# One K^TV product moved behind an output tile, W' units spread singly, a thirteenth half-tile kept in SBUF

## Chip, cores, metric

The kernel runs on one core of a Trainium2 chip. The metric is the time of one execution in microseconds (us), lower is better. A *span* is the time from the first to the last instruction of the one execution that was traced; it is about 1.3 us shorter than the timed run.

## The reference, cut to what matters

Two linear-attention branches A and B work on the same input `x` (2048 x 640, bf16, 32 heads of 20) and are mixed by a gate.

```python
qkv = x @ wqkv;  pq, pk = phi(q), phi(k)      # phi: exp below zero, t + 1 above, plus 1e-6
kv  = einsum("bhsd,bhse->bhde", pk, v)        # K^TV, one 20 x 20 block for each head
z   = sum over s of pk
o   = (pq @ kv) / (pq . z + 1e-6)
branch = o @ wo
out = g * A + (1 - g) * B                     # g = sigmoid(sum(x * gate_w))
```

## The kernel before

The kernel never forms `v`. It computes G = K^T X ("g units"), transposes G by DMA, multiplies it by the V weights (K^TV), masks the result to the head blocks on VectorE, and multiplies by `wo` to get W' ("W' units": PE, a ScalarE copy, and a DMA that rearranges the rows). An output tile of 128 rows is phi(q), scaled by the gate and the denominator, times W'. Each half of it (one branch) takes ten matmuls.

A list scheduler in the kernel, with its own cost for each instruction, fixes the order on each engine. PE alone keeps the order of the program text. The scheduler also deals out the eight banks of PSUM.

```python
def kv_unit(X):                                   # K^TV
    for us in ((0, 1, 2, 3), (4, 5)):             # 20 matmuls, then 10
        ps = Buf("kv", "ps")                      # one PSUM bank for each group
        ...  e.matmul(PS[0:GR, ps.slot, GR*i : GR*i+GR], WV[X][:, c, lo:lo+GR], gv[...])       # L661
        op("DVE", ... tensor_tensor(out=KVL[X]..., in0=PS[0:GR, ps.slot, ...], in1=BDM ...))   # the mask, L676

def wp_unit(X, u):                                # W': PE (L697, L698), ScalarE copy (L711), DMA into WP
    ...
def den(X):                                       # denominators: 4 matmuls in 4 column groups (L826)
    ...  # then ScalarE copies them from PSUM (L845), VectorE takes reciprocals (L855),
         # DMAs broadcast them, VectorE scales the phi(q) tiles (L891)

def o_part(t):                                    # first branch's half: PE (L913), ScalarE copy to OA[t] (L937)
def o_rest(t):                                    # second branch's half: PE (L913), VectorE adds OA[t] (L950)
def out_unit(t):                                  # both halves accumulated in PSUM, ScalarE copy (L959)
...
o_part(0); o_part(1); o_part(2)
den("B")
kv_unit("B")
o_part(3)
for u in range(NU):                               # NU = 6
    wp_unit("B", u)
    if u % 2:
        o_part(4 + u // 2)
for t in range(7, NOA):                           # NOA = 12
    o_part(t)
...
for t in range(NOA): o_rest(t)
for t in range(NOA, NT - 1): out_unit(t)
out_last(NT - 1)
```

`... ` and closing comments are cuts and notes of this document; `L` numbers are those of the profile.

Of the kernel before, what the change touches and what calls it, by code (L numbers as in the profile page):

```python
# [74 lines left out]
class Sched:  # L75
# [7 lines left out]
    def op(self, eng, fn, cost, ins=(), outs=(), after=(), prio=None, name="", dma=None):  # L83
        o = Op(eng, fn, cost, list(ins), list(outs), after, len(self.ops) if prio is None else prio, name, dma)
        self.ops.append(o)
        return o
# [165 lines left out]
def body(nc, A_x, A_wqkv, A_wo, B_x, B_wqkv, B_wo, gate_w, out, log=None):  # L252
# [6 lines left out]
    bf, f32 = dt.bfloat16, dt.float32  # L259
# [11 lines left out]
    PK = {X: sb("PK" + X, [128, NT * D], bf) for X in XS}  # L271
# [22 lines left out]
    GSf = GS["A"][:, :, :].rearrange("p c f -> p (c f)")  # L294
    PQ["B", 3] = GSf[:, 0:2560].rearrange("p (g s) -> p g s", g=NC)
    FXT = {"A": WV["A"][:, :, :].rearrange("p c f -> p (c f)")[:, 0:2048].rearrange("p (b s) -> p b s", b=NB), "B": XNf[:, 0:2048].rearrange("p (b s) -> p b s", b=NB)}
    NOA = 12
    OA = [XNf[:, 2048 + 1280 * i : 3328 + 1280 * i].bitcast(f32) for i in range(6)]
    OA += [PK["B"][:, 1280 * i : 1280 * i + 1280].bitcast(f32) for i in range(6)]
    NEK, NEQ, NOS = 4, 4, 4  # L300
    EK = sb("EK", [128, NEK, D], bf)
    EQ = EK[:, :, :].rearrange("p k f -> p (k f)")[:, 0 : NEQ * 512].rearrange("p (k f) -> p k f", k=NEQ)
# [27 lines left out]
    def psw(b, w):  # L330
        return PS[:, b.slot : b.slot + b.n, :].rearrange("p a b -> p (a b)")[:, 0:w]
# [15 lines left out]
    def mm_cost(n):  # L347
        return n / 2.4 + 2.5

    def act_cost(n):  # L350
        return 190 + 0.833 * n

    def dve1(n):
        return 155 + 1.04 * n
# [297 lines left out]
    def kv_unit(X):  # L652
        gv = GS[X][:, :, :].rearrange("p c (g m) -> p c g m", g=NC)
        for us in ((0, 1, 2, 3), (4, 5)):
            ps = Buf("kv", "ps")

            def fn(e, us=us, ps=ps):
                for i, u in enumerate(us):
                    lo = GR * u if u < 5 else D - GR
                    for c in range(NC):  # L660
                        r = e.matmul(  # L661
                            PS[0:GR, ps.slot, GR * i : GR * i + GR],
                            WV[X][:, c, lo : lo + GR],
                            gv[:, c, :, lo // 5 : lo // 5 + 24],
                            start=(c == 0),
                            stop=(c == NC - 1),
                        )
                return r

            op("PE", fn, 5 * len(us) * mm_cost(GR), ins=[bwv[X]] + [bgs[X, g] for g in range(NC)], outs=[ps], name="kv" + X)  # L670
            b = Buf("kvl")
            bkvl[X].append(b)
            n = len(us)
            op(
                "DVE",
                lambda e, us=us, ps=ps, n=n: e.tensor_tensor(  # L676
                    out=KVL[X][:, us[0] : us[0] + n, :].rearrange("p u (m g) -> p u g m", g=NC),
                    in0=PS[0:GR, ps.slot, 0 : GR * n].rearrange("p (u g m) -> p u g m", u=n, g=NC),
                    in1=BDM.unsqueeze(1).unsqueeze(1).to_broadcast([GR, n, NC, 24]),
                    op=ALU.mult,  # L680
                ),
                dve1(GR * n),
                ins=[ps, bcst],
                outs=[b],
                prio=-1,
                name="kvm",
            )
# [4 lines left out]
    def wp_unit(X, u):  # L692
        ps = Buf("wp", "ps", 2)

        def fn(e):
            a = psw(ps, D)
            e.matmul(a[0:GR, 0:512], KVL[X][:, u, :], WO[X][:, u, 0:512], start=True, stop=True)  # L697
            return e.matmul(a[0:GR, 512:D], KVL[X][:, u, :], WO[X][:, u, 512:D], start=True, stop=True)  # L698

        op(  # L700
            "PE",
            fn,
            mm_cost(512) + mm_cost(128),
            ins=[bkvl[X][u // 4], bwo[X] if u < 5 else bwo[X, 5]],
            outs=[ps],
            name="wp%s%d" % (X, u),
        )
        b = Buf("wst")
        op(
            "ACT",  # L710
            lambda e: e.activation(WST[X][:, u, :], psw(ps, D)[0:GR, :], ACT.Copy),  # L711
            act_cost(D),
            ins=[ps],
            outs=[b],
            prio=-1,
            name="wpc",
        )
        bwp[X, u] = b
        d = Buf("wpm")
        bwpm[X].append(d)  # L720
        r = 80 if u == 5 else 0
        lo, hi = GR * u, min(D, GR * u + GR)
        dma(
            "SP",
            "wpm%s%d" % (X, u),
            WP[X][lo // 5 : hi // 5, :, :],
            WST[X][r:GR, u, :],
            1280 * (hi - lo),
            ins=[b],
            outs=[d],  # L730
            issue=850.0,
            prio=-1,
        )
# [53 lines left out]
    def scale_now(X, b, h):  # L787
        pqs_op[X, b, h].prio = len(sch.ops)
# [116 lines left out]
    def o_mm(X, t, ps, lo, hi, first="A", last="B"):  # L905
        b = t // 4

        def fn(e):
            a = psw(ps, hi - lo)
            for g in range(NC):  # L910
                for l0 in range(lo, hi, 512):
                    h0 = min(hi, l0 + 512)
                    r = e.matmul(  # L913
                        a[:, l0 - lo : h0 - lo],
                        PQ[X, b][:, g, 128 * (t % 4) : 128 * (t % 4) + 128],
                        WP[X][:, g, l0:h0],
                        start=(X == first and g == 0),
                        stop=(X == last and g == NC - 1),
                    )
            return r  # L920

        op(
            "PE",
            fn,
            5 * sum(mm_cost(min(512, hi - l0)) for l0 in range(lo, hi, 512)),
            ins=[bfx[X, b, t % 4 // 2]] + bwpm[X],
            outs=[ps],
            name="o%s%d" % (X, t),
        )
# [3 lines left out]
    def o_part(t):  # L933
        ps, b = Buf("oa", "ps", 2), Buf("oas")
        boa[t] = b
        o_mm("A", t, ps, 0, D, last="A")
        op("ACT", lambda e: e.activation(OA[t], psw(ps, D), ACT.Copy), act_cost(D), ins=[ps], outs=[b], name="oac")  # L937

    def o_rest(t):
        ps = Buf("o", "ps", 2)  # L940
        o_mm("B", t, ps, 0, D, first="B")
        o_post(t, ps, 0, D, "ADD")
# [29 lines left out]
    def out_unit(t):  # L972
        ps = Buf("o", "ps", 2)
        for X in XS:
            o_mm(X, t, ps, 0, D)
        o_post(t, ps, 0, D, "ACT")
# [52 lines left out]
    o_part(1)  # L1029
    o_part(2)  # L1030
    den("B")
    kv_unit("B")
    o_part(3)
    for u in range(NU):
        wp_unit("B", u)
        if u % 2:
            o_part(4 + u // 2)
    for t in range(7, NOA):
        o_part(t)
    for b in range(3):  # L1040
        for h in range(2):
            scale_now("B", b, h)
    for t in range(NOA):
        o_rest(t)
    for h in range(2):
        scale_now("B", 3, h)
    for t in range(NOA, NT - 1):
        out_unit(t)
# [11 lines left out]
def bass_gated_mix__linear_attn_block__linear_attn_block__prompt_kernel(nc, *args):  # L1060
    body(nc, *args)
# [28 lines left out]
```

## Time and profile before

| | before |
|---|---|
| time, median of the first 3 runs | 191.1 us (190.75 to 191.29) |
| span of the traced execution | 189.5 us |
| PE busy | 184.9 us, 98% |
| denominator matmul of B starts | 143.83 us |
| last copy (VectorE, 128 columns) starts | 187.47 us |
| end of the span after that start | 2.04 us |

First, the page of the kernel before: the share of busy time (engine, busy us, share of the span, instructions), and the chain that ended last, by engine.

```profile
PE 184.9 (98%) x1245; PEld 108.1 (57%) x1269; DVE 127.4 (67%) x251; ACT 95.6 (50%) x171; POOL 0.4 (0%) x6
...
PE 98%; issue 1%; DVE 0%; DVEq 0%
```

PE (matmuls) is the limit. Its weight loads (PEld) run beside the matmuls. The list of waits of PE, before: who waited for whom, us in total, times, longest.

```profile
PE ps L425 <- DVE ONE L368: 1.1, 1, 1.1
PE ps L743 <- issue: 0.2, 1, 0.2
```

Next, the timeline of the stretch that the change rearranges, before. Columns: start, duration, engine, line, operation, output<-inputs, count; in brackets the idle time before it and what ended it.

```profile
143.83 0.40 PE L826 MATMUL ps<-TSH,CST 128*32 128x512 bf16 x4
...
144.16 1.89 PEld L661 LDWEIGHTS ps<-GSB,WVB 128*120 128x120 bf16 x30 [0.23 <-issue]
144.16 2.02 PE L661 MATMUL ps<-GSB,WVB 128*120 128x120 bf16 x30
144.54 0.83 ACT L845 ACTIVATE DTT<-ps,EPSC 128x256 f32<-128x256 f32 x2
145.04 0.95 DVE L855 RECIPROCAL RCT<-DTT 128x128 f32<-128x128 f32 x1 [1.45 <-ACT DTT L845]
145.91 2.10 DVE L676 TENSOR_TENSOR KVLB<-ps,CST 120x480 bf16<-120x480 f32 x2
...
147.45 0.13 PEld L697 LDWEIGHTS ps<-WOB,KVLB 120*120 120x120 bf16 x1 [0.25 <-issue]
147.48 0.40 PE L697 MATMUL ps<-WOB,KVLB 120*120 120x512 bf16 x1
```

From the denominator matmul (L826) PE goes to K^TV (L661), an output half-tile (not shown), and the first W' unit (L697). Denominator to first W' unit is 147.48 - 143.83 = 3.65 us. The "issue" entry of 0.2 us in the list of waits belongs to branch A's denominator matmul, at 106.2 us: the next matmul there (L743) starts 0.18 us late. Here PE shows no gap, but that is no proof that it did not wait: a matmul's end is modelled, and 120-column matmuls that start 0.055 us apart each carry a modelled duration of about 0.22 us, so a pause of up to 0.16 us between two of them stays covered.

### The profile page before, as it was taken

Reading aid. Unit: us, or ns where it says so; the run is one execution under the profiler, and the core shown is the slowest. Engines: PE = TensorE matmul, PEld = TensorE weight load, DVE = VectorE, ACT = ScalarE, POOL = GpSimd, SP = SyncE. Lnnn points to the kernel's source line nnn. Section 1 sums busy time; section 2 is a strip of 40 time slices with the busy share of each in tenths; the row PEclk is TensorE's granted clock in tenths of the full one; section 3 lists DMA queues with packets and bytes.
Section 4 is the critical chain, followed back from the end, with each engine's and each line's share of the span. In section 5 each row is a group of like instructions: output and inputs, shape, how many; then the busy total and the mean of one; then the engine's idle time right before and its main releaser. Section 6 shows DMA issues by size and latency. Waiting matters only on the chain.

```text
span 189.5 us, 3195 instructions
## 1 busy us (share of the span) xinstructions
PE 184.9 (98%) x1245; PEld 108.1 (57%) x1269; DVE 127.4 (67%) x251; ACT 95.6 (50%) x171; POOL 0.4 (0%) x6
## 2 busy tenths in 40 slices
PE   7999999999999999999999999999999999999995
PEld 3555555555565656655557556655666555555552
DVE  2389888888833546478787689888996935865300
ACT  2256565656554545544584777876624875000112
POOL 0000000000000000000000000000000000000000
PEclk9999999999999999999999999999999999999999
DMA  5979999999014011013010006330020053233312
GB/s 142 310 137 139 196 358 377 364 244 208 13 44 105 0 38 35 0 35 31 7 21 13 3 3 144 109 98 5 0 50 19 24 169 94 73 136 108 107 69 69
DMA packets 29469, 19.42 MB, mean 102 GB/s; under 512 B 17390, under 2 KB 29198, under 8 KB 29454
## 3 DMA queue, kind: packets, MB, share of 16 engines
q1 hardware_dynamic: 29300, 19.17, 39.2%
q8 instruction: 10, 0.16, 0.4%
q10 hardware_dynamic: 154, 0.05, 0.2%
q14 instruction: 5, 0.04, 0.1%
HBM read 9.95 MB, written 2.64 MB: 66 GB/s over the span
## 4 chain that ended last, share of the span: by engine, by line
PE 98%; issue 1%; DVE 0%; DVEq 0%
PE ps L913 23%; PE ps L743 22%; PE ps L620 18%; PE ps L491 18%; PE ps L492 5%; PE ps L621 5%; PE ps L661 2%; PE ps L425 1%; PE ps L697 1%; PE ps L438 1%; PE ps L698 0%; PE ps L826 0%; DVE TSB L957 0%; DVE ONE L368 0%; PE ps L472 0%
## 5 line engine op out<-in xcount | busy, mean ns | idle before, releaser
L491 PE MATMUL ps<-WKW,XT 128*128 128x512 bf16 x154 | 43.1, 380 | 0.0
L760 ACT ACTIVATE EK<-ps 128x512 bf16<-128x512 f32 x40 | 23.9, 599 | 31.3 <-PE ps L743 29.9
L492 PE MATMUL ps<-WKW,XT 128*128 128x128 bf16 (+1 forms) x160 | 35.2, 220 | 0.3
L524 ACT ACTIVATE EK<-ps 128x640 bf16<-128x640 f32 x32 | 22.3, 703 | 12.5 <-PE ps L492 6.1
L491 PEld LDWEIGHTS ps<-WKW,XT 128*128 128x128 bf16 x160 | 15.7, 98 | 19.0 <-issue 0.3
L743 PE MATMUL ps<-XT,WQA 128*128 128x512 bf16 x96 | 24.0, 379 | 0.1
L743 PE MATMUL ps<-XT,WQB 128*128 128x512 bf16 x95 | 23.3, 379 | 0.4 <-issue 0.2
L620 PE MATMUL ps<-XN,PKB 128*128 128x512 bf16 x80 | 23.5, 379 | 0.0
L770 DVE TENSOR_SCALAR EK<-EK 128x512 bf16<-128x512 bf16 x40 | 11.6, 291 | 17.2 <-ACT EK L760 17.0
L620 PE MATMUL ps<-XN,PKA 128*128 128x512 bf16 x78 | 23.1, 379 | 0.1
L621 PE MATMUL ps<-XN,PKA 128*128 128x129 bf16 x80 | 17.6, 220 | 0.1
L621 PE MATMUL ps<-XN,PKB 128*128 128x129 bf16 x80 | 17.6, 220 | 0.0
L913 PE MATMUL ps<-WPA,EX 128*128 128x128 bf16 (+1 forms) x116 | 16.8, 296 | 0.2
L913 PE MATMUL ps<-WPB,PKA 128*128 128x512 bf16 (+1 forms) x118 | 16.4, 298 | 0.1
L743 PEld LDWEIGHTS ps<-XT,WQB 128*128 128x128 bf16 x100 | 10.9, 118 | 8.5 <-issue 0.2
L492 PEld LDWEIGHTS ps<-WKW,XT 128*128 128x128 bf16 x160 | 15.7, 98 | 0.0
L743 PEld LDWEIGHTS ps<-XT,WQA 128*128 128x128 bf16 x100 | 10.6, 117 | 8.1
L527 DVE TENSOR_SCALAR EK<-EK 128x640 bf16<-128x640 bf16 x32 | 10.4, 325 | 7.0 <-ACT EK L524 7.0
L959 ACT ACTIVATE TSB<-ps 128x640 bf16<-128x640 f32 (+1 forms) x4 | 2.7, 677 | 23.9 <-PE ps L913 23.9
L620 PEld LDWEIGHTS ps<-XN,PKA 128*128 128x128 bf16 x80 | 9.4, 117 | 7.9
L620 PEld LDWEIGHTS ps<-XN,PKB 128*128 128x128 bf16 x80 | 9.4, 118 | 7.8
L535 DVE SCALAR_TENSOR_TENSOR PKA<-ps,EK 128x640 bf16<-128x640 f32 x16 | 13.2, 825 | 0.6
(77 smaller groups left out, 231.5 us busy)
## 6 DMA issues: line engine op xcount, KB each, us to landing
out_dram<-TSB SPq DMA_DIRECT2D x15, 160.0 KB, 1.8
XN<-in_A_x_dram SPq DMA_DIRECT2D x1, 2240.0 KB, 9.2
WKW<-in_A_wqkv_dram SPq DMA_DIRECT2D x5, 160.0 KB, 3.5
WKW<-in_B_wqkv_dram SPq DMA_DIRECT2D x5, 160.0 KB, 3.9
WQA<-in_A_wqkv_dram SPq DMA_DIRECT2D x1, 800.0 KB, 10.9
WQB<-in_B_wqkv_dram SPq DMA_DIRECT2D x1, 800.0 KB, 13.6
WVA<-in_A_wqkv_dram SPq DMA_DIRECT2D x1, 800.0 KB, 12.8
WVB<-in_B_wqkv_dram SPq DMA_DIRECT2D x1, 800.0 KB, 14.3
```

Source lines behind the costliest of these rows:

```text
L491: e.matmul(a[:, 0:512], l, WK[X][:, c, 0:512], start=(c == 0), stop=(c == NC - 1))
L492: return e.matmul(a[:, 512:w], l, WK[X][:, c, 512:w], start=(c == 0), stop=(c == NC - 1))
L524: op("ACT", lambda e: e.activation(EK[:, ek.slot, :], psw(ps, D), ACT.Exp), act_cost(D), ins=[ps] + first, outs=[ek], name="ke")
L527: lambda e: e.tensor_scalar(EK[:, ek.slot, :], EK[:, ek.slot, :], 1.0, EPS, op0=ALU.min, op1=ALU.add),
L535: lambda e: e.scalar_tensor_tensor(PKt[X][:, t, :], psw(ps, D), 0.0, EK[:, ek.slot, :], op0=ALU.max, op1=ALU.add),
L620: e.matmul(a[:, 0:512], l, XN[:, t, 0:512], start=(t == 0), stop=(t == NT - 1))
L621: return e.matmul(a[:, 512 : D + 1], l, XN[:, t, 512 : D + 1], start=(t == 0), stop=(t == NT - 1))
L661: r = e.matmul(PS[0:GR, ps.slot, GR * i : GR * i + GR], WV[X][:, c, lo : lo + GR], gv[:, c, :, lo // 5 : lo // 5 + 24], start=(c == 0), st ...
L743: r = e.matmul(PS[:, ps.slot, :], WQ[X][:, c, g::5], XT[:, c, 512 * b : 512 * b + 512], start=(c == 0), stop=(c == NC - 1),)
L760: lambda e: e.activation(EQ[:, eq.slot, :], PS[:, ps.slot, :], ACT.Exp),
L770: lambda e: e.tensor_scalar(EQ[:, eq.slot, :], EQ[:, eq.slot, :], 1.0, EPS, op0=ALU.min, op1=ALU.add),
L913: r = e.matmul(a[:, l0 - lo : h0 - lo], PQ[X, b][:, g, 128 * (t % 4) : 128 * (t % 4) + 128], WP[X][:, g, l0:h0], start=(X == first and g = ...
```

## The change

Its intent: give the transposed data of branch B one tile more to land before K^TV, have one copy of W' at a time for ScalarE, and use a free stretch of SBUF for a thirteenth first-branch half, so that one more tile of PE work can stand before the second-branch halves, which need W'.

```diff
-    NOA = 12
+    NOA = 13
-    OA += [PK["B"][:, 1280 * i : 1280 * i + 1280].bitcast(f32) for i in range(6)]
+    OA += [PK["B"][:, 1280 * i : 1280 * i + 1280].bitcast(f32) for i in range(7)]
@@
     den("B")
+    o_part(3)
     kv_unit("B")
-    o_part(3)
+    o_part(4)
     for u in range(NU):
         wp_unit("B", u)
-        if u % 2:
-            o_part(4 + u // 2)
-    for t in range(7, NOA):
+        if u % 2 == 0:
+            o_part(5 + u // 2)
+    for t in range(8, NOA):
         o_part(t)
```

## The prediction

> **What bounds the kernel now.** The matrix engine (PE). The page's first part gives it 184.9 of the 189.5 us span (98%), the windows a granted clock of 1.00 throughout. The chain of waits is 98% PE; the list of waits has 1.1 us at the start (memset) and 0.2 us elsewhere. In the timeline an output half-tile (five 512-column and five 128-column matmuls) takes 1.36 us: twelve second-branch halves fill 16.30 us without a hole (160.03 to 176.33). The Trainium skill, "TensorE: Matmul & The Clock Gate", section "Back-to-back issue gap", gives N/2.4 + 2.5 ns per isolated matmul; worked out, 5 x (215.8 + 55.8) ns = 1.36 us, so the trace agrees: these matmuls run at their own pace. The tail after the last matmul (copy, then an output DMA landing 1.6 to 1.8 us after issue) is about 2 us.
>
> **What the change does.** It removes no matmul and adds none. Tile 12 becomes two halves (first branch to SBUF, second added by VectorE) instead of one accumulation: on PE the same 2 x 1.36 us. ScalarE swaps a 0.70 us output copy for a 0.70 us copy to SBUF; VectorE gains a 0.82 us add, and has room (29% idle in the twelve halves). The thirteenth buffer lies in a part of the second branch's phi(k) whose last reader is PE work before all output tiles. So the change can only move waits.
>
> Waits it aims at, before:
> 1. From the denominator matmul to K^TV of branch B (144.2): the weight load sat 0.23 us ("issue"), and the chain gives this K^TV 1.95 us against 1.65 us for branch A's, which follows ordinary matmuls. The transposed data it reads was issued at 140.6; at the median 2.6 us it landed near 143.2, so this is mostly no wait for data. With a tile between, I estimate 0.1 to 0.2 us gained.
> 2. K^TV to the first W' unit: the mask (1.43 us, from 145.91) ended near 147.34, the unit began at 147.48 after 0.25 us of weight-load idleness. Perhaps 0.1 us lies here. After, I expect one more 0.95 us reciprocal before the mask, which still ends 0.4 us ahead.
> 3. W' units in pairs, 0.27 to 0.29 us each, then tiles at 1.36: no hole, so spreading them gains PE nothing; it smooths ScalarE (0.65 us per unit).
>
> What moves the wrong way: the last W' unit comes 2.8 us later (154.7 against 151.9), the first second-branch half only 1.36 us later (161.4). Before, the rearranging DMAs and the broadcasts kept the DMA busy until about 159.0 (windows). I estimate that the last W' rows land at 159 to 160, leaving 1.4 us or more. The first scaling of query tiles, begun at 151.4 before, is needed by 161.4.
>
> **Predicted:** 190.9 us, 80% range 190.4 to 191.4; 0.01 faster by over 2%, 0.98 within 2%, 0.01 slower. Span about 189.4 us.
>
> **What the profile would show.** Right: PE busy near 184.9 us, the chain 98% PE; K^TV of branch B at 1.65 to 1.8 us; second-branch halves from about 161.4, thirteen in 17.7 us without a hole; tiles 13 to 15 and the tail as before. Wrong: PE waiting for the W' DMA before the first second-branch half, for the mask before the first W' unit, or for the scaled last query block before half-tile 12.
>
> **What would make it wrong.** The other engines' order comes from a list scheduler with its own costs; a changed order on the SyncE queue could put broadcasts before the last W' rows and make PE wait a microsecond or two. A gain of over 0.5 us would need holes that the list of waits does not show.

## The result

| | before | after |
|---|---|---|
| median, 6 runs each | 191.0 us (190.74 to 191.29) | 190.87 us (190.69 to 191.1) |
| ratio | | 0.9995 (95%: 0.9982 to 1.0008) |
| span of the traced execution | 189.5 us | 189.5 us |
| PE busy | 184.9 us | 184.8 us |
| denominator matmul of B starts | 143.83 us | 144.16 us |
| from there to the last copy's start | 43.64 us | 43.29 us |

A ratio is the mean time of one kernel's fast runs over that of the other's of the same rounds, so it is not quite the ratio of the medians.

The last two rows say more than the times. Inside the rearranged part the changed kernel is 0.35 us shorter, and in this pair of traces it lost 0.33 us before that part began. The page after:

```profile
PE 184.8 (98%) x1245; PEld 108.3 (57%) x1269; DVE 128.6 (68%) x252; ACT 95.8 (51%) x171; POOL 0.4 (0%) x6
```

The chain, by engine, has the same shares as before. The list of waits of PE after has the same two entries as before (1.1 us on the memset, 0.2 us "issue"). The timeline of the same stretch, after:

```profile
144.16 0.40 PE L826 MATMUL ps<-TSH,CST 128*32 128x512 bf16 x4
...
144.48 1.20 PEld L913 LDWEIGHTS ps<-WPA,EX 128*128 128x128 bf16 x10 [0.23 <-issue]
144.49 1.53 PE L913 MATMUL ps<-WPA,EX 128*128 128x512 bf16 x10
144.86 0.83 ACT L845 ACTIVATE DTT<-ps,EPSC 128x256 f32<-128x256 f32 x2
145.36 1.77 DVE L855 RECIPROCAL RCT<-DTT 128x128 f32<-128x128 f32 x2 [1.45 <-ACT DTT L845]
145.80 1.73 PEld L661 LDWEIGHTS ps<-GSB,WVB 128*120 128x120 bf16 x30
145.86 1.81 PE L661 MATMUL ps<-GSB,WVB 128*120 128x120 bf16 x30
...
147.16 2.16 DVE L676 TENSOR_TENSOR KVLB<-ps,CST 120x480 bf16<-120x480 f32 x2
...
148.81 0.13 PEld L697 LDWEIGHTS ps<-WOB,KVLB 120*120 120x120 bf16 x1
148.86 0.38 PE L697 MATMUL ps<-WOB,KVLB 120*120 120x512 bf16 x1
```

Denominator to first W' unit is now 4.70 us with two output tiles between. A tile is 1.36 us, so with one tile it would be 3.34, against 3.65 before: 0.31 of the 0.35 us is gained here. Note the bracket at 144.48. The prediction expected the 0.23 us weight-load pause after the denominator matmul to be hidden by the move; it is still there, in front of the tile. Something else went.

The start of the two traces shows where 0.33 us was lost. The order of the instructions is the same in both up to the denominator matmul. Before (timeline of PE, L438 transposes the second input tile, L491 are matmuls with 512 columns):

```profile
5.06 0.65 PE L438 MATMUL ps<-CST,XN 128*128 128x128 bf16 x5
5.66 0.39 PE L491 MATMUL ps<-WKW,XT 128*128 128x512 bf16 x1
5.89 0.22 PE L492 MATMUL ps<-WKW,XT 128*128 128x128 bf16 x1
5.94 0.38 PE L491 MATMUL ps<-WKW,XT 128*128 128x512 bf16 x1
```

After:

```profile
5.05 0.71 PE L438 MATMUL ps<-CST,XN 128*128 128x128 bf16 x5
5.55 0.63 PE L491 MATMUL ps<-WKW,XT 128*128 128x512 bf16 x1
5.98 0.31 PE L492 MATMUL ps<-WKW,XT 128*128 128x128 bf16 x1
6.09 0.56 PE L491 MATMUL ps<-WKW,XT 128*128 128x512 bf16 x1
6.49 0.22 PE L492 MATMUL ps<-WKW,XT 128*128 128x128 bf16 x1
6.54 0.38 PE L491 MATMUL ps<-WKW,XT 128*128 128x512 bf16 x1
```

A matmul of 512 columns first takes 0.6 us and starts 0.43 us before its successor, later 0.38 and 0.22 us. The first of the fast ones starts at 5.66 us before and at 6.54 us after. That this is the clock is in the packed trace itself, in a record that no view prints: full clock from 5.50 us before and from 6.45 us after. (The stretch ahead of it has no entry, and the clock column of the views counts that as 1.00, so the column does not show the slow start.) The shift stays: L472 starts at 6.58 and 6.91 us, branch A's denominator matmul at 106.21 and 106.53. The Trainium skill, "TensorE: Matmul & The Clock Gate", section "What's actually happening", says that the clock is released by a free-running activity window and that the moment therefore differs from run to run of the same kernel. These two traces agree with that, and it is not an effect of the change: both programs are identical up to that point.

### The profile page after: what moved, and what is told of

Read it like the earlier page. It is cut to its first block, busy times and chain, and to the rows that moved or that the text cites. A ratio compares the mean times of both kernels' runs of the same rounds, so it can differ in the third digit from the quotient of the medians.

```text
span 189.5 us, 3196 instructions
## 1 busy us (share of the span) xinstructions
PE 184.8 (98%) x1245; PEld 108.3 (57%) x1269; DVE 128.6 (68%) x252; ACT 95.8 (51%) x171; POOL 0.4 (0%) x6
## 4 chain that ended last, share of the span: by engine, by line
PE 98%; issue 1%; DVE 0%; DVEq 0%
PE ps L913 23%; PE ps L743 22%; PE ps L620 18%; PE ps L491 18%; PE ps L492 5%; PE ps L621 5%; PE ps L661 2%; PE ps L425 1%; PE ps L697 1%; PE ps L438 1%; PE ps L698 0%; PE ps L826 0%; DVE TSB L957 0%; DVE ONE L368 0%; PE ps L472 0%
## 5 line engine op out<-in xcount | busy, mean ns | idle before, releaser
L491 PE MATMUL ps<-WKW,XT 128*128 128x512 bf16 x154 | 43.5, 383 | 0.0
L491 PEld LDWEIGHTS ps<-WKW,XT 128*128 128x128 bf16 x160 | 15.8, 98 | 19.1 <-DVE XT L453 0.5
L913 PE MATMUL ps<-WPB,PKA 128*128 128x128 bf16 (+1 forms) x117 | 16.1, 297 | 0.2
L959 ACT ACTIVATE TSB<-ps 128x640 bf16<-128x640 f32 (+1 forms) x3 | 2.0, 669 | 23.2 <-PE ps L913 23.2
L535 DVE SCALAR_TENSOR_TENSOR PKB<-ps,EK 128x640 bf16<-128x640 f32 x16 | 13.2, 825 | 0.6
```

The costliest lines, as they stand in the source:

```text
L491: e.matmul(a[:, 0:512], l, WK[X][:, c, 0:512], start=(c == 0), stop=(c == NC - 1))
L535: lambda e: e.scalar_tensor_tensor(PKt[X][:, t, :], psw(ps, D), 0.0, EK[:, ek.slot, :], op0=ALU.max, op1=ALU.add),
L913: r = e.matmul(a[:, l0 - lo : h0 - lo], PQ[X, b][:, g, 128 * (t % 4) : 128 * (t % 4) + 128], WP[X][:, g, l0:h0], start=(X == first and g = ...
```

## The experiments

Twelve runs followed the first pair, eleven of other kernels and one of the changed kernel again; all were correct. The measure is the time from the start of the denominator matmul of B to the start of the last copy, in the timeline of each trace, because it leaves out the scatter of the start. It repeats: the changed kernel gave 43.29 us in its first trace and 43.30 in a second one on another occasion. From the last copy's start to the end of the span it was 2.04 to 2.07 us in all fourteen traces. In the views all traces have a granted clock of 1.00.

| trace | denominator starts | to first W' unit | to last copy | against before |
|---|---|---|---|---|
| before | 143.83 | 3.65 (1 tile) | 43.64 | |
| after | 144.16 | 4.70 (2 tiles) | 43.29 | -0.35 |
| own banks | 144.22 | 3.66 (1) | 43.65 | +0.01 |
| two tiles | 143.96 | 4.91 (2) | 43.49 | -0.15 |
| own banks and two tiles | 143.99 | 4.74 (2) | 43.33 | -0.31 |
| K^TV later only | 144.23 | 4.71 (2) | 43.29 | -0.35 |
| spread only | 144.37 | 3.66 (1) | 43.62 | -0.02 |
| thirteen only | 144.19 | 3.66 (1) | 43.64 | 0.00 |
| no tile before W' | 144.63 | 4.63 (1) | 44.60 | +0.96 |
| W' three tiles later | 144.10 | 8.79 (5) | 44.86 | +1.22 |

The theory, formed on the two traces: (1) In the kernel before, the second group of K^TV matmuls is given the PSUM bank that the denominators were written to, so it cannot begin before ScalarE has copied them out (L845, done at 144.54 + 0.83 = 145.37 us). (2) The first W' unit waits a little for the mask. The tile put before K^TV hides the first; the mask comes earlier against the first W' unit, and that hides the second. Rivals: the weight load after the denominator matmul (the prediction's), late transposed data, the spread of the W' units, the thirteenth tile.

The hole in K^TV before, in windows of 0.1 us of K^TV alone (columns: window, length, PE busy and its matmuls, PEld busy and its loads, clock, DMA):

```profile
145.20:145.30 0.10, 0.10 (x5) 0.10 (x3) 1.00 0.00 0
145.30:145.40 0.10, 0.10 (x4) 0.03 (x1) 1.00 0.00 0
145.40:145.50 0.10, 0.10 (x3) 0.08 (x2) 1.00 0.00 0
145.50:145.60 0.10, 0.10 (x3) 0.10 (x4) 1.00 0.00 0
```

The weight loads pause right after 145.3, two thirds of the way through the thirty, and resume at about 145.4, when the copy of the denominators is done.

### Own banks

Both groups go to one free pair of banks; the order on ScalarE, VectorE and SyncE was compared and is the same as before.

```diff
-        for us in ((0, 1, 2, 3), (4, 5)):
-            ps = Buf("kv", "ps")
+        for k, us in enumerate(((0, 1, 2, 3), (4, 5))):
+            ps = ps if X == "B" and k else Buf("kv", "ps", 2 if X == "B" else 1)
...
-                            PS[0:GR, ps.slot, GR * i : GR * i + GR],
+                            PS[0:GR, ps.slot + ps.n // 2 * k, GR * i : GR * i + GR],
```

> Before's order, but both K^TV groups of branch B write one free pair of PSUM banks instead of the second group reusing the denominators' bank; the order on every other engine is unchanged. Theory (bank wait): the hole of about 0.2 us between the 20th and 21st K^TV matmul goes, K^TV takes about 1.65 us in place of 1.95; but the first W' unit still waits for the mask, so the start of the denominator matmul to the start of the first W' unit stays at 3.6 to 3.65 us. Rival 1 (the prediction's: weights loaded late after the denominator matmul): K^TV stays at 1.95. Rival 2 (transposed data late): stays at 1.95, with the hole ahead of the first K^TV matmul.

Measured: the hole is gone, and the chain of waits gives K^TV 1.79 us instead of 1.95. The rest, 0.14 us over 1.65, stays with the denominator matmul in front. The timeline:

```profile
144.22 0.40 PE L826 MATMUL ps<-TSH,CST 128*32 128x512 bf16 x4
...
144.55 1.72 PEld L661 LDWEIGHTS ps<-GSB,WVB 128*120 128x120 bf16 x30 [0.23 <-issue]
144.55 1.86 PE L661 MATMUL ps<-GSB,WVB 128*120 128x120 bf16 x30
...
146.30 2.11 DVE L676 TENSOR_TENSOR KVLB<-ps,CST 120x480 bf16<-120x480 f32 x2
...
147.85 0.13 PEld L697 LDWEIGHTS ps<-WOB,KVLB 120*120 120x120 bf16 x1 [0.42 <-issue]
147.88 0.40 PE L697 MATMUL ps<-WOB,KVLB 120*120 120x512 bf16 x1
```

The thirty loads span 1.72 us (1.89 before), so the bank wait was 0.16 to 0.17 us. And yet nothing is gained: the mask starts 2.08 us after the denominator matmul in both kernels, since a reciprocal (0.95 us) is in front of it on VectorE. The first W' unit starts 3.66 us after the denominator as ever, and its weight load now pauses 0.42 us instead of 0.25. Two paths meet at the first W' unit: on PE by K^TV and a tile, on ScalarE and VectorE by the copy, a reciprocal and the mask. The second is the longer one here, so PE gains nothing by being ready earlier. The rest of the expectation, K^TV at 1.65 us, was too low: 0.14 us is a third term.

### Two tiles

Before's order with `o_part(4)` also between K^TV and the first W' unit, and the later tiles one up.

> Before's order with a second output tile between K^TV and the first W' unit. Theory: the hole inside K^TV stays (1.95 us) and only the mask's wait goes: denominator start to first W' unit is 3.65 + 1.36 - 0.1 = 4.9 us. If there is no mask wait in before, 5.0 us.

Measured: 4.91 us, K^TV still 1.95 us in the chain, the weight load of the first W' unit without a pause, and 0.15 us less to the last copy. The wait for the mask was worth about 0.12 us by this (the chain gives the first W' matmul 0.34 us before and 0.22 here); the other 0.03 fit the tile after the first pair of W' units, which took 1.39 us before and 1.36 here in the chain.

### Own banks and two tiles

> Both of the former together. Theory: bank wait 0.2 us and mask wait 0.1 us add, denominator start to first W' unit 4.7 us with two tiles, the same as the changed kernel, though K^TV directly follows the denominator matmul. Rivals: K^TV at 1.95 us, 4.9 us or more.

Measured: 4.74 us, and -0.31 us to the last copy, with K^TV directly behind the denominator matmul. K^TV again 1.79 us in the chain. The two waits add up to 0.31 of the change's 0.35 us. The other 0.04 is the third term: after the denominator matmul the next weight load always sits 0.23 us. That costs K^TV 0.14 us (1.79 against 1.65) and an output tile 0.10 us (1.46 against 1.36 in the chain), so putting the tile there saves 0.04, not 0.14.

### Parts of the change alone

K^TV later only: `den, o_part(3), kv_unit, o_part(4)`, W' units in pairs, twelve tiles kept.

> Of the change only K^TV one tile later; W' units in pairs, twelve tiles kept. Theory: the whole gain is here: denominator start to first W' unit 4.7 us (two tiles), denominator start to the last copy 43.3 us as in the changed kernel against 43.64 before. Rival (spread or thirteenth tile give part of it): 43.4 to 43.6.

Measured: -0.35 us, all of the change's gain.

Spread only: `if u % 2 == 0: o_part(4 + u // 2)`, the rest as before.

> Of the change only the W' units spread one by one; K^TV directly after the denominator matmul, twelve tiles. Theory: nothing: denominator start to last copy 43.6 us as before. Rival (pairs of W' units hold PE up): up to 0.1 us less.

Measured: -0.02 us, which is at most the repeatability seen (0.01) and one unit of rounding: nothing.

Thirteen only: the two lines of `NOA` and `OA`.

> Of the change only the thirteenth tile kept in SBUF. Theory: nothing: denominator start to last copy 43.6 us as before, no new wait. Rival: PE waits for the scaled last query block, 43.7 or more.

Measured: 0.00 us, no new wait.

### No tile before W'

The changed kernel with `o_part(4)` moved behind the first W' unit.

> The changed kernel without the output tile between K^TV and the first W' unit (that tile is put later). Theory: the mask is not hidden any more, the first W' unit waits about 1.15 us: denominator start to first W' unit about 4.5 us with one tile (3.34 if there were no wait), and denominator start to last copy about 44.4 us. If the mask did not matter: 43.3.

Measured: 44.60 us, 1.31 more than the changed kernel. The waits of PE:

```profile
PE ps L697 <- DVE KVLB L676: 1.1, 1, 1.1
```

The first W' unit waits 1.12 us for the mask (timeline). In the changed kernel one tile after K^TV hides all of it; before, with one reciprocal fewer ahead of the mask, 0.12 us stuck out. Denominator to first W' unit was 4.63 us where 4.5 was expected, 1.29 over the 3.34 without a wait: the list starts its 1.12 us at the modelled end of the last K^TV matmul, which lies about 0.16 us behind the moment when the next could have started.

### W' three tiles later

The changed kernel with `o_part(4)` to `o_part(7)` ahead of the first W' unit. The scheduler then put all broadcasts of the denominators ahead of the W' DMAs.

> The changed kernel with all W' units three tiles later (4.1 us). It measures the slack of the rearranging DMAs before the first second-branch half, which the prediction put at 1.4 us or more. Theory (slack 2 to 3 us): PE stands 1 to 2 us before the first second-branch half, denominator start to last copy 44.3 to 45.3 us. If the slack were over 4 us: 43.3.

Measured: 44.86 us, inside the expectation. The waits of PE:

```profile
PE ps L913 <- DMA WPB<-WKW: 1.4, 1, 1.4
```

The last W' unit started 14.23 us after the denominator matmul, against 10.15 in the changed kernel: 4.08 us later. But the order on SyncE did make a difference: with no broadcast left between them, the last W' DMA was issued (end of the issue at 160.29 us against 157.15) only 3.20 us later, counted from the denominator matmul. The time to the last copy grew by 1.57 us. So the slack of the changed kernel in front of the second-branch halves is about 3.20 - 1.57 = 1.6 us (an estimate; it takes the landing after the issue as equal). The expectation had the total right, but its slack of 2 to 3 us was too high. The prediction had "1.4 us or more".

### The changed kernel again, and the start

> The changed kernel unaltered. Denominator start to last copy repeats within 0.05 us of 43.22 (chain view), while the denominator start itself can fall anywhere between 143.9 and 144.7 us as in the ten traces so far. Mean of the fast runs over before's 0.998 to 0.999 (0.35 us is 0.18%), if the start's scatter averages out over five rounds.

Measured: 43.23 us in the chain (43.30 in the timeline). Five rounds: 190.68 us median, before 190.87 (11 runs), ratio 0.9982, 95% 0.9966 to 0.9998. That is 0.34 us (0.18% of 190.9), and it agrees with the traces. The earlier ratio, 0.9995, was measured with as few runs of a start that scatters by 0.9 us over the traces (143.75 to 144.63): its interval just reaches the later value.

Without the dummy matmuls: `warm(6)` to `warm(0)` in the changed kernel.

> The changed kernel without the six dummy matmuls at the start. Theory (the clock comes up a fixed stretch after PE starts to work, and its moment makes part of the scatter of the start): PE starts 2.5 us later, so more of the first real matmuls run at 0.43 us in place of 0.216, and the denominator starts about 1.2 us later (half of 2.5), 145 to 146 us; after it nothing changes: 43.2 us to the last copy. Rival (scatter of the start comes from the loads alone): denominator start as ever, 143.9 to 144.7.

Measured: a miss. The denominator matmul started at 144.45 us, inside the range of the kernels that warm up, and 0.34 us after the mean of the other thirteen traces (144.11). PE began work at 3.35 us instead of 1.05, but the first matmul at full speed came at 7.31 us, only 0.6 to 2.9 us later than in the others (4.37 to 6.75). After the denominator it took 43.30 us, as it should.

The scatter has a second source. In "thirteen only" the clock was full from 4.38 us on, and still the denominator matmul came at 144.19 us, because the second input tile landed late:

```profile
4.38 0.38 PE L491 MATMUL ps<-WKW,XT 128*128 128x512 bf16 x1
4.59 0.22 PE L492 MATMUL ps<-WKW,XT 128*128 128x128 bf16 x1
5.37 0.45 PE L438 MATMUL ps<-CST,XN 128*128 128x128 bf16 x5 [0.56 <-DMA XN<-in_A_x_dram]
```

### Two tries at a faster version

Tail: the output DMA of the last tile's first 512 columns on ScalarE's queue.

```diff
-            o_post(t, ps, lo, hi, eng)
+            o_post(t, ps, lo, hi, eng, "ACT" if eng == "ACT" else "SP")
```

> The changed kernel with the output transfer of the last tile's first 512 columns issued on ScalarE's queue, so that the last 128 columns' issue on SyncE does not queue behind it (0.4 us an issue). Estimate: the span after the last copy's start falls from 2.05 us by 0.1 to 0.15; denominator start to last copy as in the changed kernel. In all 0.4 to 0.5 us under before, ratio near 0.9975.

Measured: 190.41 us median of 5, ratio 0.9973 (0.9956 to 0.999). But the mechanism failed: after the last copy's start the span took 2.06 us, not less than 2.04. The last issue did come earlier (it ended 0.65 us after the copy's start, 0.86 before), and the last transfer took 1.7 us to land instead of 1.6, so about half of it was given back, as far as one decimal tells; the rest is not accounted for. The two lines of landing times, before and with the edit (out<-in, queue, count, size, us to landing):

```profile
out_dram<-TSB SPq DMA_DIRECT2D x1, 32.0 KB, 1.6
```

```profile
out_dram<-TSB SPq DMA_DIRECT2D x1, 32.0 KB, 1.7
```

Its interval overlaps that of the changed kernel measured in the same rounds, and its trace has an early start (143.75) and no shorter tail. That it is faster than the changed kernel is not shown.

Front and tail: the second input tile on ScalarE's queue too.

```diff
+    ld_x("ACT", 1)
     dma("ACT", "gw", ...)
...
-        if c < 2:
+        if c < 1:
             ld_x("SP", c)
```

> The former, and the second input tile loaded on ScalarE's queue instead of third on SyncE's, to take scatter out of the start. If the second tile's late landing (its transposes began at 5.05 to 5.50 us in the traces) makes the scatter, these begin before 4.9 us and the denominator starts at 143.3 to 144.0; if the first weights are merely delayed by it in turn, no gain.

Measured: 190.72 us median of 6 (189.95 to 190.96), ratio 0.9983 (0.9964 to 1.0001). The transposes of the second tile began at 4.64 us, as wanted, and then PE waited for the weights instead:

```profile
PE ps L492 <- DMA WKW<-in_A_wqkv_dram: 0.6, 1, 0.6
```

The wait changed its name. The denominator matmul started at 143.84 us, within the range expected but also within that of the others, and the runs scatter at least as much as before.

## Why the prediction was right

The time, 190.9 us with a range of 190.4 to 191.4, held: 190.87 us. The number alone tests little, since the range holds the time without any gain too (191.0). The gain named, 0.2 to 0.3 us, came near the 0.35 us of the traces in part by luck, because a wait that was not seen stood in for one that did not go. Point by point:

- *PE bounds the kernel, and the change adds and removes no matmul.* Right. PE is busy 98% in both, and the thirteenth tile alone gave 0.00 us.
- *"The change can only move waits."* Right.
- *Wait 1, denominator matmul to K^TV.* The size was near, the cause mostly wrong. The prediction put 0.1 to 0.2 us on a weight load that is not hidden behind the denominator matmul, "mostly no wait for data". K^TV did fall from 1.95 to 1.65 us. But the pause of 0.23 us stays after the move and costs the tile 0.10 us, so moving it gives 0.04. The other 0.16 us was a hole between the 20th and 21st matmul: the wait for the denominators' PSUM bank. Own banks remove it with K^TV where it was. The step that failed is reading one pause in front of K^TV as the cause of a difference that lay inside it.
- *Wait 2, the mask.* Right: "perhaps 0.1 us", measured 0.12 to 0.15 by "two tiles". The extra reciprocal ahead of the mask came as foreseen (x2 in the timeline after). The mask ended at about 148.66 us (147.16 + 1.50), 0.15 us ahead of the load and not 0.4.
- What the prediction did not see is that the mask's path hides the first wait: with the bank wait alone removed nothing is gained (43.65 against 43.64 us). The change removes both by moving K^TV: PE gets a tile more (1.36 us) ahead of the first W' unit, while the mask starts only 0.92 us later after the denominator matmul (3.00 against 2.08), by the one reciprocal more.
- *Wait 3, pairs of W' units.* Right: -0.02 us.
- *What moves the wrong way.* Right, with a slack of about 1.6 us.
- *"A gain of over 0.5 us would need holes that the list of waits does not show."* Holes that it does not show did exist, 0.35 us of them.

Why is the result so small, then? The kernel's own plan, as its scheduler computes it, fell from 189.67 to 188.94 us. Of these 0.73 us, 0.46 are planned for the later K^TV and most of the rest (0.27) for the spread. In the plan the last transposed block lands at 143.9 us, after the denominator matmul (143.1), so that K^TV waits; in the trace K^TV ran on behind the denominator matmul, and its only pause inside was for a bank. In the same way the spread, measured alone, gave -0.02 us. So the planned gain was for waits that the chip did not have, and the 0.35 us that the chip did gain came from waits that the plan does not have: in it the second K^TV group and the first W' unit follow the PE work ahead of them at once. That both point the same way is luck. The 0.35 us is 0.18% of the time and less than half of the scatter of the start.

What stays open: nobody tried the mask ahead of the first reciprocal on VectorE in the order before, so that the reciprocal holds the mask up is read from the traces and not tested. The 0.23 us pause of the weight load after the denominator matmul was there in every trace looked at, but no run changed the denominator matmul itself, so its cause was not tested. What the dummy matmuls at the start are worth was not settled either.

## What to carry to other kernels

When PE is full in the profile, look at the weight-load row for holes in a run of small matmuls, and at what else the PSUM bank of the next group was used for. Where two paths meet, shortening the one that is not the longer shows nothing in the time (own banks: +0.01 us), and that does not prove that it had no wait; remove both. For gains below the scatter of the times, measure between two instructions that both kernels have, outside the part that scatters.

## What the Trainium skill lacked or had wrong

- "TensorE: Matmul & The Clock Gate", section "Back-to-back issue gap", says that in a stream of weight loads and matmuls the spacing is about 131 ns at N=512 and 81 ns at N=128, and that N/2.4 + 2.5 is for isolated ones. Here the isolated formula holds in the stream: a half-tile of five matmuls with 512 and five with 128 columns, each with its own weight load, took 1.36 us (5 x (131 + 81) ns would be 1.06), and 30 matmuls with 120 columns took 1.65 us, 55 ns each. (The page is of two minds: its section "Wait — 56ns, not 53.3ns?" gives 55.6 and 215.7 ns for back-to-back matmuls.)
- The same page, section "What's actually happening", gives the transition about 500 ns either way (and adds that one kernel had 6, 11 or 14 slow matmuls in different runs). Here the spread is wider than 500 ns either way: of the thirteen traces with the same dummy matmuls seven hold a record of the full clock, which begins between 5.15 and 6.60 us, and in "thirteen only", which holds none, a matmul with 512 columns already ran at full speed at 4.38 us.
- No page gives the time by which the weight load after a matmul spread over four column groups is late ("TensorEngine Tiling (Array Packing)", section "Key Properties", says without a figure that a change of tiling mode drains TensorE; no run here tests whether that is it): 0.23 us of pause here, 0.10 us of it paid by a tile of 128-column weights and 0.14 us by 120-column matmuls.
